# Row fetches two blocks ahead, another block order and a small second table in the hops; an inverse root on ScalarE in the attention

## The chip, the cores and the metric

The kernel runs on one core of a Trainium2 chip. The metric is the device time of one execution in microseconds; before the change it is 4582.58 us, the median of three runs (4579.6 to 4584.72).

## The reference

A graph of N = 10000 nodes with E = 160000 directed edges carries a 128-wide row per node. Seven hops spread the rows along the edges, and then every node runs attention over its own eight rows (the input and seven hops):

```python
h = x; toks = [x]
for _ in range(7):
    msg = h[src] * deg_inv_sqrt[src, None] * deg_inv_sqrt[dst, None]
    h = segment_sum(msg, dst, N); toks.append(h)
tok = stack(toks, axis=1)                       # (N, 8, 128)
t = layernorm(tok)
attn = softmax((t @ wq) @ (t @ wk).T / sqrt(128))
o = tok + (attn @ (t @ wv)) @ wo
r = layernorm(o)
return sum(softmax(r @ w_r) * o)                # (N, 128)
```

## The kernel before

**The graph as matrices.** Nodes lie in 79 blocks of 128. A first stage (pass A and its decoding) sorts the edges by the block of their destination and the 512-node group of their source. From that, hop 1 builds for each destination block t one matrix tile w of zeros and ones in fp8, which is kept in DRAM (GSd[t]) and read again by hops 2 to 7. It has a part that gathers (18 groups by 4 quarters of 32 slots: which source row goes to which slot) and a part that scatters (which slot adds to which of the block's 128 rows).

**The table.** The rows of the hop before, scaled, are a table of fp16 pairs (a high and a low part, 256 columns) in SBUF, tab, and once more in DRAM, tabd. There are two of each, taken in turns. The gather matmuls cover the sources 0 to 9215, blocks 0 to 71 of the table. Edges whose source lies in blocks 72 to 78, and the few that overflow a cell, are not covered; their rows are fetched from tabd by an indirect DMA, issued by GpSimd (POOL) with row numbers from oidx. A block has two such fetches of 128 rows each: og0 for the last blocks' sources, og1 for the overflow, whose places are in Sov.

**One block of a hop** (`block`, L432). Nine tiles of two groups are gathered: eight matmuls of 32 columns each write a PSUM tile p (L475), which ScalarE or VectorE copies as fp16 to eb (L478; of the nine, ScalarE takes 0, 2, 4, 5, 7 in hops 2 to 7 and all in hop 1). There are six p tiles (hops 2 to 7) and 14 eb tiles. The scatter matmuls (L446) add each eb into acc, one of two PSUM tiles. They lag by two tiles, and the closing of a block lags too: the list pend holds what is still to come. So TensorE's order in a steady block t is 72 gathers of t; four scatters of t-1; the overflow matmul of t-1 (L464), which closes acc; the first scatter of t; the matmul with og0 (L454); 13 scatters of t. Closing means that VectorE adds the halves of acc to s (L466), and fin writes the new table block: ScalarE the high part (L593), VectorE the low part and a maximum (L594, L596), a DMA from ScalarE's queue the block to tabd (L597). Then token_out multiplies s on POOL to r (L494), and SyncE's queue writes r to tok[k].

**The scale.** Ahead of each hop from the second on, the largest value of the table, spread over all partitions by two round trips from VectorE to TensorE and back (colmax, L121, and spread, L129), gives a power of two that scales the next table (L582 to L589).

**Order.** In the hops, the program's order is a priority: a planner with its own reckoning of durations lays the instructions in each engine's queue and may put one ahead of another that it takes to be ready later. It also sets the waits. Each engine then runs its queue in order. SyncE's queue carries the loads of w (five buffers) and the writes of r. In hop 1, one third of the loop builds the matrices for a later quad of blocks and one third the current block's hop.

**Attention.** Groups of 16 nodes by 8 rows fill a tile of 128 rows; 16 such groups are a supergroup, 40 in all. The order on every engine is the program's own (manual schedule). Turn i works on several supergroups at once, in four quarters q: transposes xT and products uT, values val and attention attend on TensorE with copies on ScalarE; ScalarE's squares (L823) give one layer norm's sum; VectorE's stats the other's. norms(i, i-3) makes both variances and calls rstd, which finds their inverse root on VectorE: a start from the bits of the number (L760, L761) and three rounds of three instructions (L763 to L765). read1, read2 and read3 are the read-out of older supergroups, store its output. PSUM: three tiles with tag a (for xT, uT, val), two for attend, one each for the rest.

Of the kernel before, what the change touches and what calls it, by code (L numbers as in the profile page):

```python
# [37 lines left out]
class Hops:  # L38
    def __init__(self, ctx, dp, missing, tc, x, src, dst, dis):
# [5 lines left out]
        self.tabd = [dp.tile([NT * 128, 256], F16, name=f"tabd{i}") for i in range(2)]  # L45
        self.tok = [None] + [dp.tile([NR, D], F32, name=f"tok{k}") for k in range(1, K + 1)]
# [70 lines left out]
    def colmax(self, pp, sp, col):  # L117

        nc = self.nc
        pm = pp.tile([128, 512], F32, name="pm", tag="acc")[0:1, 0:128]  # L120
# [5 lines left out]
    def spread(self, pp, m, out):  # L126
        nc = self.nc
        pb = pp.tile([128, 512], F32, name="pb", tag="acc")[:, 0:1]
# [3 lines left out]
    def pow2(self, pp, sp, col, cap):  # L132

        V = self.nc.vector
        m = self.colmax(pp, sp, col)
# [6 lines left out]
        self.spread(pp, r, q[:, 0:1])  # L142
# [173 lines left out]
    def place(self, ts, got):  # L316
# [49 lines left out]
        V.tensor_scalar(self.oidx[:, a:b, :NI], msc[:, 16:16 + n * NI].rearrange("p (g i) -> p g i", i=NI), float(NG * 512 - 1), None, op0=ALU.add)  # L366
# [61 lines left out]
    def block(self, t, w, tab, tabd, pend, lag, runs, first, evac, fin, drain=True):  # L428

        nc, V, A, T, G = self.nc, self.nc.vector, self.nc.scalar, self.nc.tensor, self.nc.gpsimd  # L430
        og = []
        for i in range(NI + 1):  # L432
            o = self.ogp.tile([128, 256], F16, name=f"og{i}")
            G.indirect_dma_start(out=o, out_offset=None, in_=tabd,  # L434
                                 in_offset=bass.IndirectOffsetOnAxis(ap=self.oidx[:, t, i:i + 1], axis=0))
            og.append(o)
        m = 257 if first else 256
        acc = []


        def scat(e, jj):
            if not acc:
                acc.append(self.pacc.tile([128, 512], F32, name="acc", tag="acc"))
            for j in range(e.shape[1]):
                J = 2 * jj + j
                T.matmul(acc[0][:, :m], w[:, J * 128:(J + 1) * 128], e[:, j, :m], start=J == 0, stop=False)  # L446
                if J == 0 and t > 0:
                    fetched()


        def fetched():
            for i in range(NI):
                W = w[:, (NG + i) * 128:(NG + i + 1) * 128]
                T.matmul(acc[0][:, :256], W, og[i], start=False, stop=False)  # L454
                if first:
                    T.matmul(acc[0][:, 256:257], W, self.ones16, start=False, stop=False)

        def over():
            if t == 0:
                fetched()  # L460
            So = self.Sov[:, t, :]
            if first:
                T.matmul(acc[0][:, 256:257], So, self.ones16, start=False, stop=False)
            T.matmul(acc[0][:, :256], So, og[NI], start=False, stop=True)  # L464
# [17 lines left out]
        for i, n in enumerate(runs):  # L482
# [3 lines left out]
            while drain and len(pend) > lag:  # L486
                pend.pop(0)()
            if i == len(runs) - 1:
                pend.append(over)
            yield  # L490

    def token_out(self, k, t, s, ct):
        r = self.fp.tile([128, 128], F32, name="r")
        self.nc.gpsimd.tensor_scalar(r, s, ct[:, t:t + 1], None, op0=ALU.mult)  # L494
# [3 lines left out]
    def run(self, ctx, nhop=K):  # L498
        tc, nc, V, A, T, G = self.tc, self.nc, self.nc.vector, self.nc.scalar, self.nc.tensor, self.nc.gpsimd
        with ExitStack() as c:  # L500
# [24 lines left out]
            def hop1(q):  # L525
                for t, w in zip(quads[q], W[q]):
                    yield from self.block(t, w, self.tab[0], self.tabd[0], pend, 2, (2, 2, 2, 3), True, lambda jj: True, fin1)
# [27 lines left out]
        with ExitStack() as c:  # L555
# [20 lines left out]
            for k in range(2, nhop + 1):  # L576
                i = k % 2
                tab, new = self.tab[i], self.tab[1 - i]
                din, dout = self.tabd[1 - i], self.tabd[i]
# [3 lines left out]
                if not last:  # L583
                    mc = self.sp.tile([128, 1], F32, name="mc")
                    V.tensor_reduce(mc, mx, axis=X, op=ALU.max)
                    V.tensor_mul(mc, mc, self.rho)
                    q = self.pow2(self.pacc, self.sp, mc, 2.0 ** 8)
                    V.tensor_mul(self.sinv, self.sinv, q[:, 1:2])
                    V.tensor_scalar(c1, self.dis2, q[:, 0:1], None, op0=ALU.mult)  # L589

                def fin(t, s, acc, k=k, ct=ct, c1=c1, mo=mo, new=new, dout=dout, last=last):
                    if not last:
# [4 lines left out]
                        nc.scalar.dma_start(dout[t * 128:(t + 1) * 128, :], new[:, t, :])  # L597
                    self.token_out(k, t, s, ct)

                for t in range(NT):  # L600
                    w = self.gsp.tile([128, (NJ + NG) * 128], F8, name="w")
                    nc.sync.dma_start(w, self.GSd[t])
                    for _ in self.block(t, w, tab, din, pend, 2, (9,), False, lambda jj: jj in (0, 2, 4, 5, 7), fin):
                        pass
# [63 lines left out]
def attention(ctx, tc, tok, out, wq, wk, wv, wo, w_r, ngrp=N // 16):  # L668
# [77 lines left out]
    V.tensor_scalar(Wv[:, 130:131], ident[:, 0:1], -1.0, 1.0 / D, op0=ALU.mult, op1=ALU.add)  # L746
    PT, AB = [], []
# [8 lines left out]
    def rstd(v):  # L756

        y, z = (sp.tile([128, 2, SG], F32, name="r" + c) for c in "yz")
        V.tensor_scalar(v, v, 1e-5, None, op0=ALU.add)  # L759
        V.tensor_single_scalar(y.bitcast(I32), v.bitcast(I32), 1, op=ALU.arith_shift_right)  # L760
        V.tensor_scalar(y.bitcast(I32), y.bitcast(I32), -1.0, float(0x5f3759df), op0=ALU.mult, op1=ALU.add)  # L761
        for _ in range(3):
            V.tensor_mul(z, y, y)  # L763
# [317 lines left out]
```

## Time and profile before

| | us |
|---|---|
| median of three runs | 4582.58 |
| the profiled execution: its time | 4621.35 |
| its span, first to last instruction | 4619.6 |
| start, pass A, decoding | 0 to 582 |
| hop 1 | 582 to 1350 |
| hops 2 to 7 | 1350 to 3866 |
| attention | 3866 to 4620 |

Busy over the span: TensorE 3902.3 us (84%), VectorE 3437.1 (74%), ScalarE 2441.3 (53%), POOL 1853.7 (40%). TensorE's granted clock is 0.961 on average. In the profile's rows PE is a matmul, PEld a weight load, DVE VectorE, ACT ScalarE, POOL GpSimd; times are microseconds from the span's start. A row in order of time gives start, length, engine, line, operation, the names written and read, the shape, how many such in a row, and in brackets how long the engine had been idle and what ended that. A row of a group gives busy time, the mean of one in nanoseconds, and the idle time ahead. The ends of matmuls are modelled.

### The profile page before, as it was taken

What the parts mean: (1) busy time and instruction counts of PE and PEld (TensorE: products, weight loads), DVE (VectorE), ACT (ScalarE), POOL (GpSimd) and SP (SyncE); (2) the same over time, 40 slices, a digit from 0 to 9 for tenths busy, and PEclk for the clock granted to TensorE, in tenths of its full rate; (3) what the DMA queues carried; (4) which work ended last, traced back from release to release, by engine and by line L of the source; (5) the groups of instructions that cost most, each with busy time, mean ns of one, the idle gap of its engine ahead of it and who ended that gap; (6) DMA issues with size and microseconds to landing.
All of it is one profiled execution on the core that took longest, in us unless ns stands there. A gap on an engine that the chain in (4) does not pass through costs nothing. (4 is left out here: it accounts for less than half of the span.)

```text
span 4619.6 us, 162387 instructions
## 1 busy us (share of the span) xinstructions
PE 3902.3 (84%) x69456; PEld 3011.4 (65%) x69456; DVE 3437.1 (74%) x7291; ACT 2441.3 (53%) x5817; POOL 1853.7 (40%) x1977
## 2 busy tenths in 40 slices
PE   0566389999979999999999899999989997999996
PEld 0566366666656676767676667666767775777775
DVE  6888899999966666666666666666665555999998
ACT  3000045555565555555555555555555555777773
POOL 0000046656644454544444444444544443222221
PEclk9877689999989999999999999999999999999998
DMA  3000044444455555555555555555554554222220
GB/s 112 1 1 1 6 142 149 147 148 147 148 170 172 168 169 161 172 170 167 162 171 170 159 169 168 169 160 170 172 161 155 156 156 114 68 68 74 65 73 11
DMA packets 313745, 591.53 MB, mean 128 GB/s; under 512 B 55032, under 2 KB 206678, under 8 KB 307766
## 3 DMA queue, kind: packets, MB, share of 16 engines
q1 hardware_dynamic: 217925, 476.45, 32.8%
q0 software_dynamic: 35392, 72.55, 5.5%
q10 hardware_dynamic: 59696, 32.08, 2.5%
q8 instruction: 544, 8.91, 0.8%
q14 instruction: 188, 1.53, 0.1%
HBM read 455.43 MB, written 125.46 MB: 126 GB/s over the span
## 5 line engine op out<-in xcount | busy, mean ns | idle before, releaser
L478 ACT CAST eb<-p 128x512 f16<-128x512 f32 x3081 | 1637.7, 595 | 947.4 <-PE p L475 919.5
L434 POOL DMA_INDIRECT og<-tabd,oidx x1106 | 1219.7, 1103 | 2005.5 <-PE acc L454 1016.5
L478 DVE CAST eb<-p 128x512 f16<-128x512 f32 x1896 | 1181.6, 684 | 732.6 <-PE p L475 722.0
L475 PE MATMUL p<-tab,w 128*32 128x256 f16 x39816 | 1495.1, 275 | 208.7 <-DVE eb L478 92.9
L475 PEld LDWEIGHTS <-w 128*32 128x32 fp8e4 x39816 | 977.0, 96 | 645.6 <-issue 602.9
L446 PE MATMUL acc<-eb,w 128*128 128x256 f16 (+1 forms) x9954 | 1349.8, 275 | 9.5 <-DVE indeg L517 8.1
L446 PEld LDWEIGHTS <-w 128*128 128x128 fp8e4 x9954 | 916.3, 98 | 269.6 <-issue 165.0
L494 POOL TENSOR_SCALAR r<-s,ctok 128x128 f32<-128x128 f32 x553 | 452.8, 819 | 152.7 <-DVE indeg L517 67.4
L593 ACT ACTIVATE tab<-s,c 128x128 f16<-128x128 f32 x395 | 158.6, 401 | 296.2 <-DVE s L466 282.7
L594 DVE SCALAR_TENSOR_TENSOR tab<-s,c,tab 128x128 f16<-128x128 f32 x395 | 138.9, 352 | 182.4 <-ACT tab L593 181.9
L466 DVE TENSOR_REDUCE s<-acc 128x128 f32<-128x256 f32 x553 | 229.8, 416 | 38.7 <-PE acc L464 38.2
L823 ACT ACTIVATE junk<-x 128x128 f32<-128x128 f32 x625 | 242.8, 396 | 0.0
L421 DVE TENSOR_TENSOR w<-dsl,iof 128x2432 fp8e4<-128x2432 f16 x79 | 212.2, 2686 | 0.0
L798 PE MATMUL pv<-Wv,xT 128*128 128x131 f32 x1250 | 173.7, 282 | 45.6 <-ACT xT L778 45.6
L881 POOL TENSOR_TENSOR p<-e,in 128x512 f32<-128x512 f32 (+1 forms) x40 | 40.8, 1020 | 419.0 <-DVE e L879 419.0
L262 ACT ACTIVATE U<-U 128x158 f16<-128x158 f32 x25 | 7.6, 302 | 378.1 <-PE U L255 378.1
L275 PE MATMUL ta<-o,ro 128*128 128x158 f16 x1250 | 124.8, 274 | 88.5 <-DVE ro L270 88.5
L798 PEld LDWEIGHTS pv<-Wv,xT 128*128 128x128 f32 x1250 | 151.6, 190 | 61.6 <-ACT xT L778 53.4
L809 PEld LDWEIGHTS po<-v,pT 128*128 128x128 f32 x1250 | 159.5, 194 | 43.3 <-issue 26.5
L275 PEld LDWEIGHTS <-ro 128*128 128x128 f16 x1250 | 119.8, 117 | 92.3 <-DVE ro L270 91.9
L809 PE MATMUL po<-v,pT 128*128 128x128 f32 x1250 | 167.3, 277 | 6.1 <-DVE o L815 6.1
L454 PE MATMUL acc<-og,w 128*128 128x256 f16 x553 | 151.9, 275 | 16.5 <-DMA og<-tabd,oidx 10.8
(260 smaller groups left out, 4350.8 us busy)
## 6 DMA issues: line engine op xcount, KB each, us to landing
w<-gsd SPq DMA_DIRECT2D x474, 592.0 KB
gsd<-w SPq DMA_DIRECT2D x79, 592.0 KB
rb<-srow SPq DMA_DIRECT2D x79, 576.0 KB
tok<-r SPq DMA_DIRECT2D x546, 64.0 KB
x<-tok SPq DMA_DIRECT2D x266, 128.0 KB
tabd<-tab ACTq DMA_DIRECT2D x395, 64.0 KB
og<-tabd,oidx POOLq DMA_INDIRECT x1106
out<-f SPq DMA_DIRECT2D x78, 64.0 KB
```

Of the source, the lines that this page charges most:

```text
L275: T.matmul(ta, ro[:, j, :, i], o12[:, j, :, i], start=j + i == 0, stop=j + i == NP)
L421: V.tensor_tensor(w[:, :NJ * 128].rearrange("p (j d) -> p j d", d=128), dsl[:, g, :, None].to_broadcast([128, NJ, 128]), self.iof1[:, None ...
L434: G.indirect_dma_start(out=o, out_offset=None, in_=tabd, in_offset=bass.IndirectOffsetOnAxis(ap=self.oidx[:, t, i:i + 1], axis=0))
L446: T.matmul(acc[0][:, :m], w[:, J * 128:(J + 1) * 128], e[:, j, :m], start=J == 0, stop=False)
L466: V.tensor_reduce(s, acc[0][:, 0:256].rearrange("p (h d) -> p d h", h=2), axis=X, op=ALU.add)
L475: T.matmul(p[32 * q:32 * q + 32, j], w[:, NJ * 128 + s * CAP:NJ * 128 + (s + 1) * CAP], tab[:, s, :], start=True, stop=True)
L478: (A.copy if evac(jj) else V.tensor_copy)(e[:, :n, 0:256], p[:, :n].rearrange("p j h d -> p j (h d)"))
L494: self.nc.gpsimd.tensor_scalar(r, s, ct[:, t:t + 1], None, op0=ALU.mult)
L593: A.activation(new[:, t, 0:128], s, AF.Copy, scale=c1[:, t:t + 1])
L798: T.matmul(p[:, g - a, :], S[i]["xT"][:, g, :], Wv, start=True, stop=True)
L809: T.matmul(p[:, g - a, :], PT[i % 2][:, g, :], S[i]["v"][:, g, :128], start=True, stop=True)
L823: A.activation(j, S[i]["x"][:, g, :], AF.Square, bias=S[i]["x"][:, g, 0:1], scale=-1.0, accum_out=S[i]["sq"][:, g:g + 1])
```

## The change

**Hops.** (1) A second, small DRAM table tabh holds blocks 72 to 78 alone; `rows` writes those blocks to both. og0 comes from tabh, with row numbers from 0 (the smallest held at 0). (2) From hop 2 on, the blocks run in the order 72 to 78, 0 to 71. (3) The fetches leave `block` and are asked for by `ahead`, for the block after next: it is called behind `begin`, which issues the matmuls with og0 and og1 as the first ones into acc, right after the gathers of the block and ahead of the waiting scatters. For the first two blocks of a hop og0 is asked for before the hop, and their og1 is multiplied at the closing (late), with tiles of its own. (4) The scale's round trips move into the first block of the hop, behind its gathers and behind its first scatters, with PSUM tiles of tag p. (5) In hop 1, r is made by ScalarE.

**Attention.** (6) The inverse root: ScalarE's ln and exp(-0.5 ln) in `root`, then one round on VectorE in place of three; a table set with both functions is loaded ahead of the loop. `norms` ends with the variances; the rest is `norms2`, a quarter later. (7) The 16 squares of a supergroup are issued in pieces of one to five between the copies, where they had been in four pieces of four. (8) read2, read3, store, a part of val, and resid for quarter 2 stand at other places; the sums over a node's rows (same_node) now come after one chunk of val, not two.

```diff
     def rows(self, i, tab, t0, t1, eng):
         eng.dma_start(self.tabd[i][t0 * 128:t1 * 128, :]..., tab[:, t0:t1, :])
+        a = max(t0, 4 * NG)
+        if a < t1:
+            o = self.tabh[i][(a - 4 * NG) * 128:(t1 - 4 * NG) * 128, :]
+            eng.dma_start(o.rearrange("(t p) w -> p t w", p=128), tab[:, a:t1, :])
...
+    def fetch(self, t, i, src, name=None):
+        o = self.ogp.tile([128, 256], F16, name=name or f"og{i}", bufs=2 if name else None)
+        self.nc.gpsimd.indirect_dma_start(out=o, out_offset=None, in_=src[0] if i == NI else src[1],
+                                          in_offset=bass.IndirectOffsetOnAxis(ap=self.oidx[:, t, i:i + 1], axis=0))
+        return o
...
-        for i in range(NI + 1):
-            o = self.ogp.tile([128, 256], F16, name=f"og{i}")
-            G.indirect_dma_start(...)
-            og.append(o)
...
+        def begin():
+            acc.append(self.pacc.tile([128, 512], F32, name="acc", tag="acc"))
+            for i in range(NI if late else NI + 1):
+                fetched(i, start=i == 0)
...
             for _ in range(n):
                 gather(jj)
                 jj += 1
-            while drain and len(pend) > lag:
+            if mid:
+                mid(0)
+            if not first:
+                begin()
+                ahead()
+            while len(pend) > lag:
                 pend.pop(0)()
+            if mid:
+                mid(1)
...
+        if k == 1:
+            self.nc.scalar.activation(r, s, AF.Copy, scale=ct[:, t:t + 1])
+        else:
+            self.nc.gpsimd.tensor_scalar(r, s, ct[:, t:t + 1], None, op0=ALU.mult)
...
+                order = [*range(4 * NG, NT), *range(4 * NG)]
+                og = [[None] * (NI + 1) for _ in order]
+                def ahead(n, og=og, order=order, din=din):
+                    if n + 2 < NT:
+                        for j in range(NI):
+                            og[n + 2][j] = self.fetch(order[n + 2], j, din)
+                    for m in range(0 if n == 0 else n + 2, min(n + 3, NT) if n >= 0 else 0):
+                        og[m][NI] = self.fetch(order[m], NI, din, "ogl" if m < 2 else None)
+                ahead(-2)
+                ahead(-1)
...
-    def rstd(v):
-        y, z = (sp.tile([128, 2, SG], F32, name="r" + c) for c in "yz")
-        V.tensor_scalar(v, v, 1e-5, None, op0=ALU.add)
-        V.tensor_single_scalar(y.bitcast(I32), v.bitcast(I32), 1, op=ALU.arith_shift_right)
-        V.tensor_scalar(y.bitcast(I32), y.bitcast(I32), -1.0, float(0x5f3759df), op0=ALU.mult, op1=ALU.add)
-        for _ in range(3):
+    A.preload_act_table_set("natural_log_exp_and_others")
+    def rstd(v, y):
+        z = sp.tile([128, 2, SG], F32, name="rz2")
             V.tensor_mul(z, y, y)
             V.scalar_tensor_tensor(z, z, -0.5, v, op0=ALU.mult, op1=ALU.mult)
             V.scalar_tensor_tensor(y, z, 1.5, y, op0=ALU.add, op1=ALU.mult)
...
+    def root(v):
+        y = sp.tile([128, 2, SG], F32, name="ry")
+        A.activation(y, v, AF.Ln)
+        A.activation(y, y, AF.Exp, scale=-0.5)
+        return y
...
+            for c in range(2 * q - 4, 2 * q - 2) if q >= 2 else ():
+                if ok(i):
+                    uT(i, c)
+                if c == 3:
+                    vy.append(root(vy[0]))
+                if ok(i + 1):
+                    squares(i + 1, *((0, 2), (2, 3), (3, 4), (4, 9))[c])
...
             if q == 2:
-                norms(i, i - 3)
-            if ok(i - 2):
+                vy = [norms(i, i - 3)]
+                if ok(i - 4):
+                    read2(i - 4)
+            if q == 3:
+                norms2(i, i - 3, *vy)
+                if ok(i - 2):
+                    resid(i - 2, 2)
+            if q != 2 and ok(i - 2):
                 resid(i - 2, q)
```

More of the change, by code (lines that the diff above doesn't have):

```diff
@@ L445, in scat, with close @@
                 J = 2 * jj + j
[L446 to L461, printed above, removed]
-            if first:
-                T.matmul(acc[0][:, 256:257], So, self.ones16, start=False, stop=False)
-            T.matmul(acc[0][:, :256], So, og[NI], start=False, stop=True)
+                T.matmul(acc[0][:, :m], w[:, J * 128:(J + 1) * 128], e[:, j, :m], start=first and J == 0,
+                         stop=J == NG - 1 and not (first or late))
+                if first and J == 0 and not lead:
+                    for i in range(NI):
+                        fetched(i)
+        def close():
+            if first:
+                if lead:
+                    for i in range(NI):
+                        fetched(i)
+                T.matmul(acc[0][:, 256:257], self.Sov[:, t, :], self.ones16, start=False, stop=False)
+            if first or late:
+                T.matmul(acc[0][:, :256], self.Sov[:, t, :], og[NI], start=False, stop=True)
             s = self.fp.tile([128, 128], F32, name="s")
@@ L526, in hop1 @@
                 for t, w in zip(quads[q], W[q]):
[L527 removed]
+                    og = [self.fetch(t, j, (self.tabd[0], self.tabh[0])) for j in range(NI + 1)]
+                    yield from self.block(t, w, self.tab[0], og, pend, 2, (2, 2, 2, 3), True, lambda jj: True, fin1, t == 0)
             for _ in self.place(quads[0], dsl[0]):
```

105 lines of the change are left out of this document (61 added, 44 removed).

## The prediction

> **What bounds the kernel now.** I read the busy time by stage first, and then, inside the stages that the change touches, the rows of single engines in order of time.
>
> ```profile
> 582.00:1350.00 768.00, 691.63 (x12248) 508.78 (x12245) 720.09 (x1079) 442.99 (x923) 450.22 (x244) 0.97 0.46 146
> ...
> 2196.00:2611.00 415.00, 383.81 (x7270) 288.14 (x7258) 267.50 (x565) 239.93 (x474) 203.85 (x237) 1.00 0.54 167
> ```
>
> The columns after the length are PE, PEld, DVE, ACT and POOL busy. Hop 1 (582 to 1350) is VectorE's: 720 of 768 us. Hops 2 to 7 are alike, about 417 us each with 79 blocks; nothing there is busy throughout but TensorE, and its 384 us hide waits. One block on TensorE, from one first gather to the next:
>
> ```profile
> 2403.39 1.38 PE L475 MATMUL p<-tab,w 128*32 128x256 f16 x43
> 2404.96 0.61 PE L475 MATMUL p<-tab,w 128*32 128x256 f16 x13 [0.19 <-issue]
> 2405.76 0.62 PE L475 MATMUL p<-tab,w 128*32 128x256 f16 x16 [0.19 <-DVE eb L478]
> 2406.31 0.61 PE L446 MATMUL acc<-eb,w 128*128 128x256 f16 x4
> 2406.76 0.27 PE L464 MATMUL acc<-og,Sov 128*128 128x256 f16 x1
> 2406.87 0.27 PE L446 MATMUL acc<-eb,w 128*128 128x256 f16 x1
> 2406.98 0.27 PE L454 MATMUL acc<-og,w 128*128 128x256 f16 x1
> 2407.09 1.58 PE L446 MATMUL acc<-eb,w 128*128 128x256 f16 x13
> 2408.60 0.62 PE L475 MATMUL p<-tab,w 128*32 128x256 f16 x16
> ```
>
> A block lasts 2408.60 - 2403.39 = 5.21 us: 2.92 us until the first scatter (72 gathers in three pieces, with two stops), then 2.29 us for 20 scatter-like matmuls without a stop. So the gathers' part is where time is lost. What POOL does meanwhile:
>
> ```profile
> 2402.10 1.01 POOL L434 DMA_INDIRECT og<-tabd,oidx  x1 [2.28 <-PE acc L454]
> 2403.41 0.94 POOL L434 DMA_INDIRECT og<-tabd,oidx  x1 [0.30 <-issue]
> 2404.39 0.62 POOL L494 TENSOR_SCALAR r<-s,ctok 128x128 f32<-128x128 f32 x1
> ```
>
> One fetch starts 1.29 us before the gathers, the second 0.02 us after their start. And VectorE, which takes the second gathered tile out of PSUM:
>
> ```profile
> 2405.01 1.89 DVE L478 CAST eb<-p 128x512 f16<-128x512 f32 x3 [1.38 <-PE p L475]
> ```
>
> The second tile is done with the 16th gather; 43 start within 1.38 us less one's own 0.27, 0.026 us each, so the 16th has started by 2403.81, yet VectorE hears of them only at 2405.01. The trace holds two blocks that tell whose fault that is. The last block of hop 3 has no second fetch:
>
> ```profile
> 2190.71 2.15 PE L475 MATMUL p<-tab,w 128*32 128x256 f16 x72
> 2192.79 0.39 PE L446 MATMUL acc<-eb,w 128*128 128x256 f16 x2
> ```
>
> ```profile
> 2189.42 1.01 POOL L434 DMA_INDIRECT og<-tabd,oidx  x1 [2.27 <-PE acc L454]
> 2190.46 0.77 POOL L494 TENSOR_SCALAR r<-s,ctok 128x128 f32<-128x128 f32 x1
> ```
>
> All 72 gathers run in one piece and the first scatter comes after 2.08 us, although POOL's r overlaps their start. In another block POOL was late, and both fetches fell among the gathers:
>
> ```profile
> 1524.30 1.83 PE L475 MATMUL p<-tab,w 128*32 128x256 f16 x52
> 1526.56 0.38 PE L475 MATMUL p<-tab,w 128*32 128x256 f16 x5 [0.43 <-issue]
> 1527.31 0.64 PE L475 MATMUL p<-tab,w 128*32 128x256 f16 x15 [0.38 <-issue]
> 1527.89 0.28 PE L446 MATMUL acc<-eb,w 128*128 128x256 f16 x1
> ```
>
> ```profile
> 1524.48 1.01 POOL L434 DMA_INDIRECT og<-tabd,oidx  x1 [3.76 <-issue]
> 1525.79 0.94 POOL L434 DMA_INDIRECT og<-tabd,oidx  x1 [0.30 <-issue]
> ```
>
> There the gathers took 1527.89 - 1524.30 = 3.59 us. So: no fetch among the gathers 2.08 us, one 2.92, two 3.59. While POOL works on a row fetch, TensorE's finished tiles are reported late, PSUM comes free late, and TensorE stops. This, 0.84 us in each of 6 x 79 = 474 blocks, is the largest thing the change can touch.
>
> Attention (from 3866) is VectorE's: 93.8 us of every 100, and its list of waits has no row of VectorE.
>
> ```profile
> 4066.00:4166.00 100.00, 90.96 (x1562) 75.28 (x1561) 93.82 (x354) 77.18 (x290) 23.97 (x40) 1.00 0.25 70
> ```
>
> **The blocks of hops 2 to 7.** The number of matmuls, evictions and fetches stays. In the new block the two fetched-row matmuls come first after the gathers, and the two fetches for the block after next stand behind them, ahead of the closing of the block before. Now the first fetch starts 0.99 us after the scatters' start (2401.11 in the block before, 5.20 ahead of 2406.31), which is 0.54 us after L464 (0.45 into the scatters) or 0.32 us after L454 (0.67 into them): one of the two releases it. With these matmuls at the front it starts 0.32 to 0.54 us into the scatters, the second 1.31 us later, at 1.63 to 1.85. The scatters last 2.29 us, so the second fetch starts 0.66 to 0.44 us ahead of the next gathers. What that costs the trace does not show; it lies between a fetch 1.29 us ahead (cost 0) and one 0.02 us behind (0.84). On the straight line between them the cost is 0.40 to 0.54. I take the later start and 0.55, because a fetch that waits for its own buffer's reader has the longer way: 0.84 - 0.55 = 0.29 us gained, 474 x 0.29 = **137 us**. The ends are 0 (nothing gained) and 398 us (0.84 whole). POOL's r is now behind both fetches, as it is in the rows above, and ends about as early as before relative to the scatters; who waits for it is SyncE's token write, with the weight loads queued behind it, which have five buffers. The close of a block comes one matmul (0.11 us) later, and its report can now be late by the hold of the first fetch; that delays the reduction on VectorE, which has until the first eviction of the next block, so I cost it at nothing; without that cover it would be up to 0.4 us, which eats the gain.
>
> **The seams between hops.** A hop takes 417 us and 79 x 5.20 = 411, so a seam costs some 6 us: TensorE waits for fetches of a table just written and for the scale's round trip. Afterwards the seven last blocks go first and their rows lie in a small table of their own, so the first fetches need nothing that is fresh; the scale's round trips lie behind gathers and scatters. What is late next is the overflow rows: three fetches in a row must wait for the last table row and then fall among the second block's gathers, at 0.67 to 0.84 each. I take 3.4 us left of 6: 5 x 2.6 = **13 us** gained, between 0 and 30. The extra table writes are 7 issues a hop on ScalarE's queue, which has the time (240 of 415 us busy).
>
> The seam from hop 1 to 2 gets worse:
>
> ```profile
> 1372.70 1.00 POOL L434 DMA_INDIRECT og<-tabd,oidx  x1 [11.72 <-DMA w<-gsd]
> ...
> 1375.38 0.37 PE L454 MATMUL acc<-og,w 128*128 128x256 f16 x1 [0.61 <-DMA og<-tabd,oidx]
> ```
>
> Here everything waits for the table's writing, the small table comes behind it on SyncE's queue (7 blocks on 79, 9% of a write of some 20 us: 2 us), and the first block's scatters (14 x 0.11 us) now stand behind the fetched rows and no longer before them: **4 us** lost, between 1 and 8.
>
> **Hop 1.** Its multiplication r moves from POOL to ScalarE, 443 of 768 us busy: hidden by VectorE's 720. Were that cover gone, 79 activations of some 0.4 us would cost 32 us.
>
> **Attention.** Of three rounds for the inverse root one is left, and the integer start is gone:
>
> ```profile
> 4203.98 0.24 DVE L951 TENSOR_REDUCE rz<-re 128x16 f32<-128x128 f32 x1
> ...
> 4204.76 0.17 DVE L913 TENSOR_TENSOR rx<-v 128x16 f32<-128x16 f32 x1
> ...
> 4207.01 0.27 DVE L760 TENSOR_SCALAR ry<-rv 128x32 int32<-128x32 int32 x1
> ...
> 4209.04 0.19 DVE L763 TENSOR_TENSOR rz<-ry 128x32 f32<-128x32 f32 x1
> ```
>
> VectorE loses 4209.04 - 4207.01 = 2.03 us of each turn. In 400 us (4060 to 4460) there are 23 turns, 17.39 us each; VectorE alone would need 15.36. ScalarE gets two small activations, not above this one each:
>
> ```profile
> L870 ACT ACTIVATE e<-e 128x128 f32<-128x128 f32 x23 | 7.1, 310 | 12.8 <-DVE e L864 12.8
> L798 PEld LDWEIGHTS pv<-Wv,xT 128*128 128x128 f32 x736 | 89.2, 190 | 37.0 <-ACT xT L778 32.5 <-issue 4.6
> ```
>
> Together 0.6 us at most, in a chain from VectorE to ScalarE and back; the three instructions of the read-out moved into that gap (4203.98 to 4204.76) cover 0.78, if ScalarE is free when the sums are ready, which the squares' new places, fewer ahead of it, allow. If it isn't, VectorE waits for up to a copy of 0.5 us. The second row shows the next bound: TensorE's only large idle time in those 23 turns is 37.0 us, 1.61 a turn, so TensorE cannot go under 17.39 - 1.61 = 15.78. I take 16.0, a gain of 1.4 us a turn (between 0.5 and 1.63). VectorE is the bound for about 600 us, 34.5 turns: 48 us; with the ends of the stage 52, less one table load:
>
> ```profile
> L165 ACT ACT_TABLE_LOAD x1 | 1.3, 1283 | 21.3 <-issue 21.3
> ```
>
> **51 us** gained. The page "ScalarE: Activation LUTs" of the Trainium skill (What ACT_TABLE_LOAD costs) puts a switch of table sets at 1283 ns plus a drain of about 1380; the row agrees with the first figure, and no row here shows the second. Its section on table sets lists a set that holds both exp and ln, which the change loads ahead of the loop; by that rule no turn pays a load.
>
> **Sum.** -137 - 13 + 4 - 51 = -197 us. The profiled execution itself took 4621.35 us, so 4424; the runs' median is 4582.58/4621.35 = 0.9916 of it: **4387 us**.
>
> **The rivals.**
> - B, the fetches leave the gathers' way altogether: 0.84 x 474 = 398, -458 in all, 4128 us. For it: a fetch 1.29 us ahead costs nothing. Against: the second one has only 0.44 to 0.66.
> - C, nothing is gained in the blocks: the late reports only move, to the closing of a block and the first eviction, or the planner leaves the fetches where they are, so that the change doesn't do what it says: -60, 4523 us.
> - D, slower: on POOL the planner puts r ahead of the two fetches. r needs the reduced block, so both fetches start among the gathers, as in the block at 1524.30: +0.67 x 474 = 318, less 60: 4838 us. It decides as soon as the second fetch starts later than 0.02 us after the gathers. For it: r and the fetches are ready within a microsecond of each other. Against: in the rows above the planner put fetches for later blocks ahead of r.
> - E, attention gains nothing, since ScalarE answers late or loads tables in every turn (two loads of 1283 ns inside the chain that VectorE waits for, 2.57 us where 2.03 are saved): -137 - 13 + 4 = -146, 4438 us. With the drain that the Trainium skill's page gives, an estimate, it would be 2 x 2.66 = 5.3 us a turn.
>
> **Chances.** Forecast 0.58, B 0.07, C 0.17, D 0.10, E 0.08. The range 4240 to 4540 leaves out B and D and holds the rest, with attention at both its ends. No change means within 0.2%, 9 us, about what a measurement of this kernel can tell. Slower: D and a sliver of C, 0.11; same 0.03; faster 0.86.
>
> **What would show it.** Right: on POOL a fetch starting about 0.5 us after the first matmul behind the gathers and the second 1.3 us on; gathers in 2.6 us, blocks of 4.9; the first eviction by VectorE some 1.1 us after the first gather instead of 1.62; hops of 385 to 395 us; attention turns of 16 us in which TensorE's weight loads no longer wait; two table loads in all. Wrong: r between or ahead of the fetches, gathers of 2.9 us or more, a new wait of TensorE for fetched rows in every block, or VectorE waiting for ry in every turn.

## The result, and the profile after

The changed kernel takes 4388.32 us (median of 4 runs, 4387.9 to 4391.36), the kernel before 4583.65 beside it: a ratio of 0.9577, 95% interval 0.956 to 0.9593. The forecast was 4387. Its sum is looked at below, since not every term of it was right. The profiled execution took 4388.44 us, its span is 4386.5.

Busy time by stage in the changed kernel (hop 1, one of hops 2 to 7, the middle of attention); columns as in the prediction:

```profile
582.00:1350.00 768.00, 690.18 (x12302) 505.94 (x12301) 724.47 (x1083) 467.67 (x1007) 274.57 (x165) 0.98 0.47 148
2150.00:2540.00 390.00, 378.69 (x7290) 289.68 (x7288) 268.07 (x565) 234.06 (x476) 205.02 (x239) 0.99 0.57 180
3860.00:4260.00 400.00, 395.17 (x6569) 321.51 (x6568) 380.74 (x1336) 353.92 (x1313) 105.83 (x175) 1.00 0.26 74
```

Hop 1 is VectorE's as before. A hop is some 389 us instead of 417. In attention TensorE is now busy 395 of 400 us, VectorE 381: the bound has changed over, as forecast. One block on TensorE, in order of time:

```profile
2301.06 2.62 PE L492 MATMUL p<-tab,w 128*32 128x256 f16 x72
2303.61 0.28 PE L454 MATMUL acc<-og,w 128*128 128x256 f16 x1
2303.72 0.27 PE L454 MATMUL acc<-og,Sov 128*128 128x256 f16 x1
2303.83 2.13 PE L468 MATMUL acc<-eb,w 128*128 128x256 f16 x18
2305.89 0.29 PE L492 MATMUL p<-tab,w 128*32 128x256 f16 x4
```

A block lasts 2305.89 - 2301.06 = 4.83 us, its gathers 2303.61 - 2301.06 = 2.55. POOL beside it:

```profile
2299.33 1.01 POOL L439 DMA_INDIRECT og<-tabh,oidx  x1 [1.77 <-PE acc L454]
2300.64 0.95 POOL L439 DMA_INDIRECT og<-tabd,oidx  x1 [0.30 <-issue]
2301.62 0.63 POOL L521 TENSOR_SCALAR r<-s,ctok 128x128 f32<-128x128 f32 x1
2304.16 1.01 POOL L439 DMA_INDIRECT og<-tabh,oidx  x1 [1.92 <-PE acc L454]
```

The first fetch starts 0.55 us after the first matmul behind the gathers (2304.16 against 2303.61), the second 0.42 ahead of the next gathers, and r stands behind both: rival D did not come about. VectorE's first eviction in this block:

```profile
2300.75 0.35 DVE L627 SCALAR_TENSOR_TENSOR tab<-s,c,tab 128x128 f16<-128x128 f32 x1 [0.47 <-ACT tab L626]
...
2302.24 1.89 DVE L495 CAST eb<-p 128x512 f16<-128x512 f32 x3 [0.94 <-PE p L492]
```

That is 1.18 us after the first gather, where 1.1 was forecast. ScalarE beside it (ACTq is the DMA queue that it issues to):

```profile
2301.14 0.33 ACTq L156 DMA_DIRECT2D tabd<-tab  x1
2302.15 2.05 ACT L495 CAST eb<-p 128x512 f16<-128x512 f32 x4 [1.43 <-PE p L492]
```

| stretch, to the last reduction of each stage (profiled executions) | before | after | gained | forecast |
|---|---|---|---|---|
| to the end of hop 1 | 1342.7 | 1337.5 | 5 | 0 |
| hops 2 to 7 | 2522.2 | 2352.9 | 169 | 146 |
| of these: 474 blocks at the median step (one reduction to the next) | 5.19 | 4.83 | 171 | 137 |
| of these: seam from hop 1 to 2 | 34.6 | 40.6 | -6 | -4 |
| attention | 754.6 | 696.1 | 58 | 51 |

These sum to 233 us, as the two spans do (4619.6 - 4386.5), while the medians lie 195 apart: the profiled execution of before was 38 us above its median, that of after is not.

### The profile page after: what moved, and what is told of

Its sections match the earlier page's. It is cut to its first block, busy times and chain, and to the rows that moved or that the text cites. A ratio compares the mean times of both kernels' runs of the same rounds, so it can differ in the third digit from the quotient of the medians.

```text
span 4386.5 us, 162053 instructions
## 1 busy us (share of the span) xinstructions
PE 3836.6 (87%) x69456; PEld 3003.0 (68%) x69456; DVE 3383.4 (77%) x6923; ACT 2453.6 (56%) x5989; POOL 1680.0 (38%) x1898
## 4 chain that ended last, share of the span: by engine, by line
PE 56%; ACT 6%; DVE 3%; issue 1%; DMA 1%; SPq 0%; another core or an unknown queue 0%; ACTq 0%; DVEq 0%; POOLq 0%
PE acc L468 21%; PE p L492 20%; ACT eb L495 5%; PE acc L454 3%; PE pv L842 3%; PE po L853 3%; PE pu L831 3%; PE pt L821 1%; DVE eb L495 1%; PE ps L873 1%; PE pf L1021 1%; PE sm L879 1%; DMA og<-tabh,oidx 1%; DVE st L948 0%; SPq L734 0%
## 5 line engine op out<-in xcount | busy, mean ns | idle before, releaser
L495 ACT CAST eb<-p 128x512 f16<-128x512 f32 x3081 | 1598.5, 600 | 935.5 <-PE p L492 878.9
L492 PE MATMUL p<-tab,w 128*32 128x256 f16 x39816 | 1437.7, 275 | 111.1 <-ACT eb L495 35.1
L468 PE MATMUL acc<-eb,w 128*128 128x256 f16 (+1 forms) x9954 | 1244.5, 274 | 13.1 <-DVE indeg L544 8.8
L439 POOL DMA_INDIRECT og<-tabh,oidx x553 | 631.9, 1143 | 1628.7 <-PE acc L454 868.7
L468 PEld LDWEIGHTS <-w 128*128 128x128 fp8e4 x9954 | 954.6, 98 | 174.6 <-issue 59.6
L439 POOL DMA_INDIRECT og<-tabd,oidx x541 | 557.4, 1030 | 457.5 <-PE acc L481 276.3
L521 POOL TENSOR_SCALAR r<-s,ctok 128x128 f32<-128x128 f32 x474 | 297.4, 627 | 40.0 <-DVE s L483 25.5
```

The lines of the kernel that those rows point to most:

```text
L439: self.nc.gpsimd.indirect_dma_start(out=o, out_offset=None, in_=src[0] if i == NI else src[1], in_offset=bass.IndirectOffsetOnAxis(ap=self ...
L492: T.matmul(p[32 * q:32 * q + 32, j], w[:, NJ * 128 + s * CAP:NJ * 128 + (s + 1) * CAP], tab[:, s, :], start=True, stop=True)
L495: (A.copy if evac(jj) else V.tensor_copy)(e[:, :n, 0:256], p[:, :n].rearrange("p j h d -> p j (h d)"))
```

## Experiments

The runs came in four groups, each with the kernel before beside it. The first group was to take the prediction's two halves apart and to move the fetches. In it the kernel before takes 4259.86 us instead of 4583 (7 runs, 4254.05 to 4262.75). That turned the question round, so it comes first. "Chip" below means the chip of a group of runs; whether it is the chip that makes the difference stays open. All diffs are against the changed kernel.

**The two halves.** One kernel has the hops of after and the attention of before, one the reverse; each hunk of the diff is taken whole from its side. The first lines of each are shown.

```diff
-    A.preload_act_table_set("natural_log_exp_and_others")
...
-    def rstd(v, y):
...
+    def rstd(v):
...
```

> The hops of the changed kernel with the attention of the kernel before. If the prediction's terms add: 4388 + 51 to 58 = 4439 to 4446 us, attention turns 17.4 us, hops as in the changed kernel. If attention's gain is partly made by earlier ends of the hops: nearer to 4400.

Measured: 4212.65 us, ratio 0.9893 (0.9877 to 0.991), that is 47 us under before.

```diff
-    def block(self, t, w, tab, og, pend, lag, runs, first, evac, fin, lead=False, late=False, mid=None, ahead=None):
+    def block(self, t, w, tab, tabd, pend, lag, runs, first, evac, fin, drain=True):
...
```

> The hops of the kernel before with the attention of the changed kernel. If the terms add: 4583 - 51 to 58 = 4525 to 4532 us, attention turns 16.0 us, hops of 417. If the profiled execution of the kernel before was long in its hops by chance (its time lies 38 us above its median), hops here shorter than 417, near 411.

Measured: 4206.77 us, ratio 0.9881 (0.9864 to 0.9897), 53 us under before. Attention does what was forecast (its stretch is 698.8 us against 753.5 in the other kernel), but the hops of after gain only 47 us in all, and not in the blocks. A block of the kernel before's hops in this run, TensorE and then POOL and VectorE:

```profile
2303.75 2.15 PE L475 MATMUL p<-tab,w 128*32 128x256 f16 x72
2305.83 0.61 PE L446 MATMUL acc<-eb,w 128*128 128x256 f16 x4
...
2308.12 0.29 PE L475 MATMUL p<-tab,w 128*32 128x256 f16 x4
```

```profile
2302.46 1.01 POOL L434 DMA_INDIRECT og<-tabd,oidx  x1 [1.46 <-PE acc L454]
2303.77 0.95 POOL L434 DMA_INDIRECT og<-tabd,oidx  x1 [0.30 <-issue]
```

```profile
2304.42 1.89 DVE L478 CAST eb<-p 128x512 f16<-128x512 f32 x3 [0.54 <-PE p L475]
```

The fetches start 1.29 us ahead of the gathers and 0.02 behind their start and last 1.01 and 0.95 us, all as in the profile of before. Yet VectorE hears of its tile after 0.67 us instead of 1.62, the gathers run in one piece, and a block takes 4.37 us. So here a row fetch holds no report back, and there is nothing to gain in the blocks. (The delay of the reports is called the hold below.) TensorE's granted clock doesn't explain the difference: it is 0.954 in this run and 0.961 in the profile of before.

What the hops gain here lies elsewhere: 37 us in hop 1 (its last reduction at 1360.6 before, 1323.2 after) and 3.5 us at each of five seams, less 6 at the seam from hop 1 to 2. In hop 1 VectorE waits for rows, by the list of waits between 782 and 982 us of the attention-only kernel:

```profile
DVE w L418 <- DMA rb<-srow: 7.7, 4, 2.3
DVE lo L397 <- PE msc L394: 5.8, 3, 2.6
```

In the hops-only kernel's list the only wait of VectorE is 0.2 us. SyncE's queue brings these rows behind the token writes, which wait for r, so r's move may be the cause; it was not run alone on such a chip.

**The fetches left out, and the second one late.**

```diff
+                    if n > 0:
+                        if n + 2 < NT:
+                            og[n + 2][:] = og[2]
+                        return
```

> Hops 2 to 7 of the changed kernel issue no row fetch on POOL from the second block of a hop on; those blocks multiply the rows fetched for the third block once more, so the fetched rows' part of the sums is left out. All matmuls, evictions and writes stay. Theory (a row fetch on POOL holds back TensorE's reports): the gather part falls from 2.49 to 2.08 us, a block from 4.83 to 4.4 (474 x 0.4 = 190 to 220 us), 4170 to 4200 in all. Rival (the gain of the change came from where the fetched-row matmuls stand, and the fetches' place is indifferent): gather part 2.49 and 4388 as before.

```diff
+        if e is not None:
+            self.nc.scalar.copy(o[:, 0:1], e[:, 0, 0:1])
...
+                def second(n, e, og=og, order=order, din=din):
+                    if 1 <= n < NT - 1:
+                        og[n + 1][NI] = self.fetch(order[n + 1], NI, din, None, e)
```

> The changed kernel, but the second fetch of a block no longer stands behind the first: it is issued once the next block's first gathered tile is evicted, some 1.4 us into the gathers (a 128x1 copy on ScalarE into its buffer makes it wait). Theory (what costs is a fetch that starts between about 0.5 us ahead of the gathers and their middle, because reports are held some 1.5 us from its start, and a start at 1.3 us is too late to harm): gathers in one piece, blocks of 4.4 us, 474 x 0.4 = 190, less some for the copy, 4190 to 4250. Rival (any fetch among the gathers costs 0.67 to 0.84): blocks of 5.2, 4388 + 474 x 0.4 = 4570.

Measured: 4157.38 us without the fetches and 4189.81 with the second late, blocks of 4.37 and 4.42 us. The first lies 13 us below the range that the theory gave, the second at the lower end of its range, and neither tells anything: the kernel before was itself at 4.37. A forecast met, or nearly met, for another reason is no evidence.

**The changed kernel once more, and six variants in one.** The changed kernel was run again, and beside it a kernel that has another variant in each hop, so that one execution compares them.

> The changed kernel itself, once more. The four runs so far were on a chip on which the kernel before takes 4260 us and its blocks in hops 2 to 7 take 4.37 us with the two row fetches in the very same places (1.29 us ahead of the gathers, 0.02 us behind their start) that cost 0.84 us a block in the profile of before. Theory H (whether a fetch holds back TensorE's reports depends on the chip, the kernel's other costs do not): on a chip where before takes 4260, 4155 to 4165 (ratio 0.976 to 0.978: hop 1 37, seams 13 - 6, attention 55 gained, blocks 0); on a chip where before takes 4583, 4388 (0.957). Rival (the four runs on that chip differ only by chance): ratio 0.957 again wherever it runs.

Measured: 4396.44 us against 4586.87, ratio 0.958 (0.9564 to 0.9596). The hold is there again.

```diff
+                order = [*range(4 * NG, NT), *range(4 * NG)] if k not in (5, 6) else list(range(NT))
...
+                            og[n + 2][j] = self.fetch(order[n + 2], j, din, far=k == 6)
...
+                    if k == 7 and n >= 0:
+                        self.fetch(order[n], 0, din, "ogx")
...
+                    if k == 5:
+                        og[n] = [self.fetch(t, 0, din, far=True), self.fetch(t, 1, din)]
```

> The changed kernel with another variant in each hop: hop 2 as changed; hop 3 issues no fetches from its second block on (the rows of the third block are multiplied again, so the fetched rows' part of this hop is wrong); hop 4 issues the second fetch only once the next block's first gathered tile is evicted; hop 5 has the order of blocks, of matmuls and the fetches' places of the kernel before; hop 6 the order of blocks of before and all rows from the large table; hop 7 a third fetch in every block, which nobody reads. Theory (a fetch holds TensorE's reports) on a chip that shows it: blocks of 4.83, 4.4, 4.4 to 4.5, 5.2, 4.83 and 5.2 or more in hops 2 to 7. Rival (the order of the matmuls made the gain there): 4.83, 4.83, 4.83, 5.2, 4.83, 4.83. On a chip that does not: 4.37 in all, 4.42 in hop 4; hop 6 then shows the seam by itself, about 3 us longer than hop 2's.

Measured: median blocks of 4.84, 4.37, 4.73, 5.12 and 4.84 us in hops 2 to 6 (whole kernel 4480.67). A block of hop 3 (no fetch) and one of hop 5 (as before) on TensorE, each with the next one's first gather:

```profile
2003.90 2.15 PE L502 MATMUL p<-tab,w 128*32 128x256 f16 x72
...
2008.27 0.29 PE L502 MATMUL p<-tab,w 128*32 128x256 f16 x4
...
2600.04 2.11 PE L502 MATMUL p<-tab,w 128*32 128x256 f16 x56
2602.34 0.62 PE L502 MATMUL p<-tab,w 128*32 128x256 f16 x16 [0.19 <-DVE eb L505]
2602.90 0.61 PE L475 MATMUL acc<-eb,w 128*128 128x256 f16 x4
...
2605.18 0.29 PE L502 MATMUL p<-tab,w 128*32 128x256 f16 x4
```

In one execution on one chip, then: no fetch 4.37, which is what every block takes where nothing is held; before's places 5.12; the changed places 4.84. The rival (the order of the matmuls made the gain) is out: hop 3 has the new order too, and where nothing is held both orders take 4.37. The late second fetch costs 0.36 over no fetch, more than expected. In hop 7 the planner put the 79 extra fetches, which nobody reads, into its first 19 blocks, some six fetches in each; blocks there took 7 to 13 us with POOL as the bound, so this hop prices nothing. Hop 6, with the old order and one table, is 391.5 us against 390.6, 388.8, 389.8 and 389.7 for hops 3 to 6 of the changed kernel: its seam is some 2 us longer.

**More buffers.** If a fetch need not wait for its buffer's reader, it can start sooner.

```diff
-            self.ogp = c.enter_context(tc.tile_pool(name="og2", bufs=2))
+            self.ogp = c.enter_context(tc.tile_pool(name="og2", bufs=3))
```

> The changed kernel with three buffers instead of two for the fetched rows. The two fetches of a block then need not wait for the matmul that reads their buffer; on POOL they start right behind r, some 1.2 and 2.5 us after the block's first gather, the second 1.8 us ahead of the next gathers instead of 0.41. Theory (a fetch holds back TensorE's reports for about 1.6 us from its start, which is costly only while the first tiles of a block are due): on a chip where before takes 4583, blocks of 4.4 to 4.5 us instead of 4.83, 4388 - 474 x 0.33 to 0.43 = 4184 to 4232 us. Rival (any fetch among the gathers costs 0.67 to 0.84): 5.2 us and 4560. On a chip where before takes 4260 no change: 4155 to 4165.

```diff
+        if r is not None:
+            self.nc.gpsimd.tensor_copy(o[:, 0:max(1, wait)], r[:, 0:max(1, wait)])
```

> As the kernel with three buffers, but each fetch is tied to r by a copy of one column on POOL into its buffer, so that it cannot start ahead of it. Theory: as with three buffers, and what the copies take on POOL (some 0.2 us a block) costs nothing. Rival (the fetches' place behind r is not kept without the tie): this one is faster than the one with three buffers.

```diff
+                        if k in (5, 7):
+                            og[n + 2][0] = self.fetch(order[n + 2], 0, din, "ogs" if k == 5 else None)
...
+                        og[m][0] = self.fetch(order[m], 0, din, None, r, {3: 64, 4: 128}.get(k, 0))
```

> Three buffers for the rows, and another variant in each hop. Hops 2, 3 and 4: both fetches behind r, with 0, some 0.35 and some 0.65 us of a copy on POOL ahead of them, so first starts of about 1.3, 1.6 and 1.9 us after the first gather. Hop 5: only the first fetch of a block, at its place in the changed kernel (behind the fetched-row matmuls); hop 6: only the second, there; the other rows of these two hops are those of the third block again, so their sums are wrong. Hop 7: three buffers alone. Theory on a chip that shows the hold: 4.4, 4.45 and 4.6 us (the second fetch comes nearer to the next gathers), 4.37 in hops 5 and 6 (a lone fetch 1.7 us ahead of the gathers costs nothing), 4.4 in hop 7. Rival (each fetch costs the same wherever it is): 4.83 in hops 2, 3, 4 and 7, 4.6 in hops 5 and 6.

These three ran where before takes 4260.72 us: 4156.01 (ratio 0.975), 4194.03 and 4184.47 us, all median blocks 4.37. So they leave the theory on the fetches' places untested. The edit of the first does not do what it says:

```profile
2302.48 1.01 POOL L439 DMA_INDIRECT og<-tabh,oidx  x1 [1.45 <-PE acc L454]
2303.79 0.95 POOL L439 DMA_INDIRECT og<-tabd,oidx  x1 [0.30 <-issue]
```

The fetch still waits for the fetched-row matmul: the planner uses the third buffer to fetch one block further ahead (the last fetch of hop 7 starts 14.1 us ahead of the last reduction, against 9.8 in the hops-only kernel), and it starts behind that matmul all the same. The changed kernel itself was not run where nothing is held. This kernel does the same work with its fetches at the same places of a block, so it stands for it: 105 us under before, against 195 on a chip with the hold. Tying the fetches to r cost 38 us there, in single blocks of 5 to 6 us.

**The fetches' places, on a chip with the hold.** The last run puts the fetches of each hop in another place. The kernel before takes 4590.98 us beside it.

```diff
+                        if k == 4:
...
+                                G.tensor_copy(o[:, 128 * j:128 * j + 128], self.ident)
...
+                        if k == 3:
+                            og[n + 2][1] = og[2][1]
...
+                def gate(n, jj, by, k=k):
+                    if n > 0 and jj == k - 6:
+                        tied(n + 2, by)
```

> The changed kernel with hop 1's r back on POOL and another place of the row fetches in each hop. Hop 2: as changed. Hop 3: only the first fetch of a block, at its place. Hop 4: only the second, its place kept by two copies on POOL in the first one's stead (in hops 3 and 4 the rows that are not fetched are wrong). Hop 5: both behind r, some 0.6 and 1.9 us after the first gather. Hops 6 and 7: both behind the eviction of the block's first or second gathered tile, some 1.6 or 2.0 us after the first gather, and 1.3 us later. Theory, on a chip where before takes 4583 (a fetch holds reports for 1.6 us from its start, and the first tiles' reports are what TensorE waits for): 4.83 us a block in hop 2, 4.37 in hop 3, 4.8 in hop 4, 4.9 or more in hop 5, 4.4 to 4.6 in hop 6, 4.7 in hop 7 as with the late second fetch. Rival (each fetch costs its 0.23 us wherever it is): 4.83 but in hops 3 and 4, 4.6 there. On a chip where before takes 4260: 4.37 everywhere, and hop 1 ends 37 us later than in the changed kernel if r on POOL was what the move to ScalarE mended.

Measured: 4347.09 us in all; median blocks 4.84, 4.37, 4.37, 5.31, 4.42 and 4.52 us in hops 2 to 7 (hop 6 uneven, 4.67 in the mean). Hop 4 on TensorE, the lone fetch on POOL:

```profile
2353.89 2.15 PE L494 MATMUL p<-tab,w 128*32 128x256 f16 x72
...
2358.25 0.40 PE L494 MATMUL p<-tab,w 128*32 128x256 f16 x8
```

```profile
2357.01 1.01 POOL L441 DMA_INDIRECT ogt<-tabd,oidx  x1 [0.17 <-PE acc L470]
```

A lone fetch 1.24 us ahead of the gathers costs nothing; the copies ahead of it were shorter than meant, so its place in the pair (0.42) was not reached. With 4.37 in hops 3 and 4, "each fetch costs its 0.23" is out. Hop 5 corrects my theory. POOL, VectorE and TensorE there:

```profile
2698.04 1.01 POOL L441 DMA_INDIRECT ogb<-tabh,oidx  x1 [0.43 <-POOL ogb L440]
2699.35 0.95 POOL L441 DMA_INDIRECT ogb<-tabd,oidx  x1 [0.30 <-issue]
```

```profile
2700.82 0.69 DVE L497 CAST eb<-p 128x512 f16<-128x512 f32 x1 [1.28 <-PE acc L470]
2701.43 0.42 DVE L485 TENSOR_REDUCE s<-acc 128x128 f32<-128x256 f32 x1
```

```profile
2699.45 2.13 PE L470 MATMUL acc<-eb,w 128*128 128x256 f16 x18
2701.51 1.49 PE L494 MATMUL p<-tab,w 128*32 128x256 f16 x48
```

The fetches fall on a block's last gathers. VectorE gets the last tile only at 2700.82, 1.47 us after the second fetch's start; the reduction at 2701.43 and the table work behind it then stand where the next block's first evictions are due, its gathers beginning at 2701.51. So late tiles matter as early ones do. The second fetch of the changed kernel gives the same length: 2300.64 to VectorE's 2302.24 is 1.60, and to ScalarE's first eviction in that block (2302.15) 1.51. By these figures two fetches 1.31 apart hold some 2.8 us of each block (an estimate), and the scatters offer 2.29. The best place measured with both is hop 7's, where the first fetch starts 2.37 us after the first gather in the median: its stretch is 363.4 us against 385.5 for hop 7 of the changed kernel run again. Put into all six hops that would be some 130 us on a chip with the hold, but this was not run by itself, and hop 7 alone writes no new table, so the other five may gain less. It also shows hop 1 with r on POOL: it ends at 1339.5.

**Attention's edits, one by one.**

```diff
+        for _ in range(3):
...
-        A.activation(y, v, AF.Ln)
-        A.activation(y, y, AF.Exp, scale=-0.5)
+        V.tensor_single_scalar(y.bitcast(I32), v.bitcast(I32), 1, op=ALU.arith_shift_right)
+        V.tensor_scalar(y.bitcast(I32), y.bitcast(I32), -1.0, float(0x5f3759df), op0=ALU.mult, op1=ALU.add)
```

> The changed kernel with two edits undone: hop 1's multiplication r back on POOL, and the inverse root in three rounds with the integer start on VectorE instead of ln and exp on ScalarE and one round. Theory: the attention turn goes from 16.0 back to 17.4 us (+48), since VectorE is the bound again; hop 1 is 5 us longer where VectorE waits for nothing else, and 37 us longer on the chip of the runs so far, where VectorE then waits 12 us in 400 for rows that SyncE's queue brings, behind the token write that waits for r. Rival for attention (the squares' spread made the gain): turn of 16.0 to 16.4.

```diff
-                    squares(i, 9, 11)
...
-                if ok(i + 1):
-                    squares(i + 1, *((0, 2), (2, 3), (3, 4), (4, 9))[c])
+            if ok(i + q // 2):
+                squares(i + q // 2, 4 * ((q + 2) % 4), 4 * ((q + 2) % 4) + 4)
```

> The changed kernel with the 16 squares of a turn in four groups at the four places of before. If their spread is what lets ScalarE answer in time: the turn goes from 16.0 to 16.3 to 16.6 (+10 to +20 us). If the spread is worth nothing: 16.0 and within 0.2%.

Measured on the chip of the second run of the changed kernel: 4457.49 us (+61) and 4412.89 (+16). One reduction of each turn gives its length. First before, then after, then three rounds on VectorE, then the old squares (count of turns, then the first and last start):

```profile
L890 DVE TENSOR_REDUCE w<-y x24: 302/303/304, 4060.8 to 4462.1; 128x16 f32<-128x144 f32 x24
```

```profile
L934 DVE TENSOR_REDUCE w<-y x26: 302/303/304, 3875.7 to 4279.6; 128x16 f32<-128x144 f32 x26
```

```profile
L932 DVE TENSOR_REDUCE w<-y x22: 302/303/304, 3870.2 to 4244.3; 128x16 f32<-128x144 f32 x22
```

```profile
L934 DVE TENSOR_REDUCE w<-y x24: 302/303/304, 3864.5 to 4247.7; 128x16 f32<-128x144 f32 x24
```

The turns are 401.3/23 = 17.45, 403.9/25 = 16.16, 374.1/21 = 17.81 and 383.2/23 = 16.66 us. The move of the root is worth 1.65 us of a turn and without it the other edits cost 0.36; the squares' spread is worth 0.5, and 0.57 is what VectorE then waits in each of 24 turns for the root, where the changed kernel has no such wait:

```profile
DVE rz L808 <- ACT ry L974: 13.6, 24, 0.6
```

Hop 1 with r on POOL ended at 1337.6, no later than in the changed kernel (1342.4 there).

## Why the prediction was right, and where it was not

**What bounds the kernel, and why.** Right for the chip of the profile: a row fetch on POOL holds back TensorE's reports. Blocks of 4.37 without fetches and 5.12 with before's places, in one execution, show it. What one profile could not tell is that in other groups of runs nothing is held back.

**Blocks, -137.** The mechanism was right: places, gathers and first eviction came as worked out. The profiled executions give 0.36 us a block, 171 in all, where 0.29 was forecast. The step that was off is the start: 5.19 us was that execution's block, while before's arrangement took 5.12 in the later run. 474 x 0.07 = 33 us would be most of the 38 by which that profiled execution lies above its median. That they lay there is only argued; if so, the term was right for the timed runs, since 5.12 - 4.83 is 0.29. Both prices in it were too high by nearly the same amount, which is luck: measured in one execution against no fetch, before's places cost 5.12 - 4.37 = 0.75 where 0.84 was taken, and the changed places 4.84 - 4.37 = 0.47 where 0.55 was. The straight line between two prices was a guess that came out; the runs show a hold of some 1.5 us from a fetch's start in its place.

**Sum times 0.9916.** This step failed in its form, for the changed kernel's profiled execution took its own median. The terms sum to 197 us, 36 less than the 233 that the profiles show; the factor took 37 off again. So the forecast time is met within 2 us by luck, by two errors that cancel. Against the timed gain of 195 the 197 look exact, but there too terms cancel: the seams' 13 did not come, and attention and hop 1 gave 7 and 5 more.

**Seams, -13.** Wrong here: taking 79 median blocks from the hop leaves 6.6 us before and 6.2 after, in the mean of hops 3 to 7. The step "three fetches in a row" failed. In the changed kernel five stand there, POOL first (first and last), then TensorE:

```profile
2146.31 0.95 POOL L439 DMA_INDIRECT ogl<-tabd,oidx  x1 [2.58 <-DMA tabd<-tab]
...
2151.31 0.95 POOL L439 DMA_INDIRECT og<-tabd,oidx  x1 [0.30 <-issue]
```

```profile
2145.78 2.16 PE L492 MATMUL p<-tab,w 128*32 128x256 f16 x57
...
2150.52 0.44 PE L492 MATMUL p<-tab,w 128*32 128x256 f16 x4 [0.44 <-issue]
2150.89 0.40 PE L468 MATMUL acc<-eb,w 128*128 128x256 f16 x1
```

These gathers take 5.11 us. In the hops-only kernel, with the same five fetches but where nothing holds, they take 2.28 and a seam gains 3.5.

**Seam 1 to 2, +4.** Measured 6 (34.6 to 40.6), inside 1 to 8; no run takes its two parts apart.

**Hop 1, 0.** Right with the hold (5 us between the profiles, and r back on POOL gave no loss in two runs). Without it the hop gains 37, which no term had and whose cause is only argued.

**Attention, -51.** Measured 58: turns of 16.16 us with TensorE as the bound, 39 x 1.25 = 49 of it by the first and last turn of the stage, the rest at its end. The cover named for the root, ScalarE free in time through the squares' spread, is shown: without it VectorE waits 0.57 us a turn, the 0.5 that was named. Rival E is out; the stage loads one table, at its start, and no turn pays:

```profile
3704.89 1.28 ACT L795 ACT_TABLE_LOAD   x1 [16.44 <-DMA x<-tok]
```

The section on table sets of the Trainium skill's page "ScalarE: Activation LUTs", cited in the prediction, counts one load for ln and then exp, since one set has both; this trace agrees, with one load for 40 turns.

## What to carry to other kernels

Compare the stop of a busy engine with what unrelated engines do at that moment, and look for the few blocks in which the coincidence is missing: two odd blocks gave the cause here, and its price within 0.1 us a block, before anything was run. Then ask whether the cause belongs to the program or to where it ran; this change is worth 4.2% in one group of runs, and a kernel with its blocks 2.5% in another. Variants in one execution, one per hop, can be compared all the same.

## What had not been expected of the hardware

When POOL issues a row fetch, TensorE's reports are held up to some 1.5 us from the fetch's start, in two of the four groups of runs after the first result; in the other two, with fetches of the same length at the same places, they are not (4.37 against 5.12 to 5.20 us a block). It stays the same for all runs of a group. The chip bore the same number, 15, in one group with it and one without, so it goes by more than that number; what decides it stays open.

The traces also hold the times of the semaphore updates, which are the reports themselves; no row above shows them. In the block of the attention-only kernel shown above (first gather at 2303.75), TensorE's nine come from 2304.18 on, 0.22 us apart. In the block of the changed kernel (first gather at 2301.06) the first five come at 2302.12, 2302.22, 2302.31, 2302.40 and 2302.50, 0.09 to 0.10 apart. The matmuls of these five tiles start at the same times in both blocks, the fifth tile's 0.88 us after the first gather, so the tiles had been waiting to be reported: it is the reports that are late and not the matmuls.

The other engines' reports are not late. In the same block VectorE is done with the low part at 2300.75 + 0.35 = 2301.10, and ScalarE's queue starts the DMA that needs it at 2301.14, 0.50 us after the second fetch's start, when TensorE is being held. Nor is it the moving of the rows that holds: in hop 4 of the run with the fetches' places, by the DMA packets in its trace, those of the lone fetch before the one shown start from 2354.96 to 2355.76, amid the gathers that begin at 2353.89 and run in one piece. So the hold belongs to the issue on POOL, about 1.0 us, and some 0.5 us behind it; by what way is open.

The section "SBUF: two separate sides" of the Trainium skill's page "SBUF — State Buffer" has POOL contend with VectorE alone, over their shared port to SBUF, and TensorE wait for nobody there; the runs with the hold show that a fetch of POOL can delay TensorE's reports, by a way that this rule does not cover.
